# Squares kept in memory by 32 rows, in runs of 512 bytes (attention and mixture of experts, one core)

## The chip, the core and the metric

The kernel runs on one core of one Trainium2 chip. The metric is device time in microseconds, the median of several executions of the compiled program. The engines are named as in the profile: PE multiplies matrices, DVE (VectorE) and ACT (ScalarE) work element by element, POOL scatters rows, and SP issues nearly all DMA transfers from one queue that it works off in order. A core has 16 DMA engines, and all transfers share them.

## The reference

```python
# 8 batches, S = 2496 rows, u and v 256 wide, z 64 wide
scores = matmul(z, z.transpose(0, 2, 1)) / S
attn = maximum(scores, 0.0) ** 2
x = (u * matmul(attn, v)).reshape(8 * 2496, 256)
logits = x @ w_gate + modality_bias[modality_id]     # 8 experts
e_idx = argmax(logits, axis=1)                       # one expert for each row
out[rows of e] = gate * (maximum(x @ w1[e], 0) @ w2[e])   # 256 -> 1024 -> 256, gate = softmax at e
```

The scores are z times its own transpose, so `attn` is symmetric: the squares of one block above the diagonal are those of the mirrored block below it, turned.

## The kernel before, in words

**Tiles.** A batch's 2496 columns (queries) are cut into five column chunks, four of T = 512 and a last one of 448 (`NCH`, `LAST`). The text calls them columns 0 to 4. The rows (keys) are taken two tiles of 128 at a time: ten steps i = 0 to 9 (`NI`) for each column, key chunk i // 2, its first or second half i % 2. The host interleaves keys so that partition p holds keys 2p and 2p + 1 of a half. `steps` lists (batch, column, i), 400 in all, in the order in which `order_of` mixes them.

**A step.** Fresh steps multiply z with z on PE (`scores`, L334), take relu and scale on ACT (`root`, L345), and square on ACT (`square`, L394). This gives `a`, 128 partitions x 2 key tiles x 512 queries in float32. `a` is split for the multiplication into a high part `ah` (`high`, L418, on DVE or ACT, whichever the scheduler finds free) and a low part `al` (`low`, L427, on DVE; L429 and L430 in the last step), and `weigh` (L451) adds ah·vh, ah·vl and al·vh into PSUM, 24 half-height matmuls a step. `ah` and `al` have `DEPTH` = 4 buffers each, `a` has `NA` = 6.

**Turned steps.** Where the mirrored block was made in an earlier column of the batch, it is not made again. The earlier step is a source (`is_source`): `turn_squares` (L364) transposes `a` in 32 x 32 blocks on DVE into one of two `turn` buffers, `store_squares` (L377, L381) writes it to memory, and the later step's `load_turned` (L354) reads it back as its `a`. Column c makes 8 - 2c full source steps and reads 2c turned ones. Below column 4 there is also a half step on the diagonal: its upper 256 queries are made (`root` writes them into the tile that `load_turned` filled), its lower 256 come from memory, stored by the step before it (i == 2c). In the last batch fewer pairs are turned.

**Layout in memory before.** `squares[q, c, e]` is 512 x 512 floats, a row for each query of the source. A source step fills 256 of a row's 512 places. Each quarter of 32 partitions goes out in a DMA of its own, 32 x 16 runs of 64 floats (256 bytes). In step 9, whose second key tile is not interleaved, runs are 32 floats (128 bytes) and there are six DMAs. A read takes 128 partitions, each two whole rows: 4096 bytes on end, or two runs of 1792 bytes in the last column, or two of 1024 in a half step.

**What sets the order.** `step_pieces`, `chunk_pieces` and others describe all work as pieces, each with an engine, a cost, a step by which it is needed, what it must follow and which buffers it takes. A list scheduler runs through them at build time with a clock for each engine and issues, for the engine that is furthest behind, the piece with the earliest need that is ready and fits. The recorded order on each engine is fixed then; the chip waits where the costs were wrong. `transfer` makes a piece of SP's queue. Besides squares the queue carries `zr` and `vr` (the next batch's z and v, mostly read in columns 2 and 3), `ut` (u), and in the first batch eight `blank` stores. POOL scatters each batch's rows (`xs`) during columns 1 to 3 of the next.

**Afterwards** (from about 1279 us) the experts run: `up` (L1268), `down_high` (L1279), `down_low` (L1283). They touch none of this.

## Time and profile before

| | |
|---|---|
| median of 3 executions | 2155.69 us (2152.55 to 2157.73) |
| the profiled execution's own time | 2161.44 us |
| its span, first to last instruction | 2159.0 us |
| mean granted PE clock | 0.995 |
| PE, weight loads, DVE, ACT busy | 2128.9, 1900.2, 1650.3, 1422.8 us |
| DMA packets, MB moved | 605497, 373.21 |

The page shows busy time of each engine over the span, and the same in slices. The table of busy time by stretch gives, for a stretch between two times, its length, busy us of PE, of PE's weight loads, DVE, ACT and POOL with their instruction counts, the granted PE clock (1.00 is full), the mean busy share of the 16 DMA engines (over 1 where packets overlap on an engine) and GB/s. Groups of instructions give count, busy us, the mean ns of one, and the idle time just before them with what ended it. The list of waits gives who waited for whom: us in total, times, longest. The chain that ended last is followed back from the last instruction to whatever released each step; its pieces give start and length in us.

### The profile page before, as it was taken

To read this page: it belongs to the slowest core of one execution; us is meant where nothing else is said; L and a number is where in the kernel's file an instruction comes from. 1 tells how busy PE (TensorE), PEld (TensorE's weight loads), DVE (VectorE), ACT (ScalarE), POOL (GpSimd) and SP (SyncE) were. 2 spreads that over 40 slices of the span, in tenths; PEclk is the share of its full clock that TensorE was granted. 3 is DMA by queue.
4 is the path that set the end of the run, shared out by engine and by line. 5 is a ranking of instruction groups with operands and counts; after the bars stand their busy time and mean duration, and the time that the engine had idled before them with its cause. 6 is when DMAs were issued, how large, how long until landed. Compare 5 with 4: busy or idle time off the path is not lost.

```text
span 2159.0 us, 44814 instructions
## 1 busy us (share of the span) xinstructions
PE 2128.9 (99%) x17190; PEld 1900.2 (88%) x17190; DVE 1650.3 (76%) x2292; ACT 1422.8 (66%) x2031; POOL 351.5 (16%) x342
## 2 busy tenths in 40 slices
PE   9999999999999999999999999999999999999997
PEld 7889999989989988888999988888888888888886
DVE  8889888878889889888888876666666666666664
ACT  8668868869768769779778753455455555454553
POOL 0000220210220210210310503112121211112121
PEclk9999999999999999999999999999999999999999
DMA  8976977977877978968968843645454544545451
GB/s 180 260 229 140 236 215 145 233 204 147 222 213 145 232 208 168 240 188 176 251 167 177 240 123 98 179 121 163 127 161 133 145 149 132 161 126 166 120 156 36
DMA packets 605497, 373.21 MB, mean 173 GB/s; under 512 B 522810, under 2 KB 547642, under 8 KB 605274
## 3 DMA queue, kind: packets, MB, share of 16 engines
q1 hardware_dynamic: 590186, 329.06, 60.8%
q0 software_dynamic: 15088, 41.21, 5.1%
q8 instruction: 136, 2.23, 0.4%
q14 instruction: 87, 0.71, 0.1%
HBM read 237.84 MB, written 132.31 MB: 171 GB/s over the span
## 4 chain that ended last, share of the span: by engine, by line
PE 86%; DMA 4%; issue 3%; DVE 3%; ACT 2%; SPq 1%; POOL 0%; POOLq 0%; DVEq 0%; ACTq 0%
PE acc L451 41%; PE ph L1268 18%; PE po L1279 12%; PE s L334 6%; PE po L1283 6%; DMA out_dram<-y,ids 2%; PE po L547 2%; DMA squares<-turn 1%; DMA r<-squares 1%; DVE al L427 1%; SPq L377 1%; ACT r L345 1%; ACT r L394 1%; DVE turn L364 0%; SPq L381 0%
## 5 line engine op out<-in xcount | busy, mean ns | idle before, releaser
L451 PE MATMUL acc<-ah,vh 64*128 64x512 f32 (+1 forms) x3120 | 468.6, 386 | 3.5 <-DVE ah L418 3.3
L451 PE MATMUL acc<-al,vh 64*128 64x512 f32 (+1 forms) x3120 | 456.5, 383 | 3.9 <-DVE al L427 3.9
L451 PE MATMUL acc<-ah,vl 64*128 64x512 f32 (+1 forms) x3120 | 455.9, 383 | 0.0
L427 DVE TENSOR_TENSOR al<-r,ah 128x1024 fp32r<-128x1024 f32 (+1 forms) x359 | 421.4, 1184 | 37.5 <-ACT ah L418 32.4
L1268 PE MATMUL ph<-xh,w 128*128 128x512 f32 x1248 | 399.5, 390 | 0.1
L1273 DVE SCALAR_TENSOR_TENSOR hl<-ph,hh 128x512 fp32r<-128x512 f32 x312 | 211.4, 688 | 236.3 <-ACT hh L1272 209.9
L1272 ACT ACTIVATE hh<-ph 128x512 fp32r<-128x512 f32 x312 | 187.1, 600 | 303.3 <-PE ph L1268 236.1
L671 POOL DMA_INDIRECT xs<-x,sloti x160 | 193.8, 1211 | 1076.4 <-ACT ah L418 492.6
L451 PEld LDWEIGHTS acc<-al,vh 64*128 64x128 f32 x3120 | 342.0, 185 | 28.6 <-DVE al L427 5.1
L451 PEld LDWEIGHTS acc<-ah,vh 64*128 64x128 f32 x3120 | 337.2, 185 | 28.7 <-DVE ah L418 3.7
L451 PEld LDWEIGHTS acc<-ah,vl 64*128 64x128 f32 x3120 | 337.3, 185 | 23.6
L418 ACT CAST ah<-r 128x1024 fp32r<-128x1024 f32 (+1 forms) x281 | 285.7, 1033 | 78.9 <-PE acc L451 46.6
L1279 PE MATMUL po<-w,hh 128*128 128x512 f32 x1248 | 296.7, 389 | 0.0
L345 ACT ACTIVATE r<-s 128x1024 f32<-128x1024 f32 (+2 forms) x244 | 235.7, 967 | 83.8 <-PE s L334 72.4
L1268 PEld LDWEIGHTS ph<-xh,w 128*128 128x128 f32 x1248 | 234.6, 188 | 47.8 <-issue 0.6
L1279 PEld LDWEIGHTS po<-w,hh 128*128 128x128 f32 x1248 | 234.1, 188 | 48.3
L1292 POOL DMA_INDIRECT out_dram<-y,ids x157 | 152.7, 973 | 721.2 <-DVE y L1320 686.2
L364 DVE STREAM_TRANSPOSE turn<-r 128x1024 f32<-128x1024 f32 (+1 forms) x189 | 217.0, 1151 | 41.1 <-DMA squares<-turn 27.6
L394 ACT ACTIVATE r<-r 128x1024 f32<-128x1024 f32 (+2 forms) x243 | 242.8, 999 | 5.7
L1268 PE MATMUL ph<-xl,w 128*128 128x512 f32 x624 | 243.7, 391 | 0.1
L334 PE MATMUL s<-zm 64*128 64x512 f32 (+2 forms) x1452 | 211.9, 383 | 5.2 <-ACT r L345 4.9
L869 DVE TENSOR_TENSOR w<-wq,w 128x1024 fp32r<-128x1024 f32 x148 | 177.8, 1221 | 19.3 <-ACT w L865 19.0
(158 smaller groups left out, 2013.1 us busy)
## 6 DMA issues: line engine op xcount, KB each, us to landing
wq<-in_moe_w_dram SPq DMA_DIRECT2D x148, 512.0 KB
squares<-turn SPq DMA_DIRECT2D x508, 128.0 KB
r<-squares SPq DMA_DIRECT2D x96, 512.0 KB
r<-squares SPq DMA_DIRECT2D x62, 448.0 KB
ut<-in_ut_dram SPq DMA_DIRECT2D x40, 512.0 KB
xg<-xs SPq DMA_DIRECT2D x156, 128.0 KB
squares<-turn SPq DMA_DIRECT2D x310, 64.0 KB
vr<-in_v_dram SPq DMA_DIRECT2D x32, 512.0 KB
```

Source lines behind the costliest of these rows:

```text
L334: nc.tensor.matmul(out=s[t][:, w], lhsT=lhs, rhs=mv[halves[t], ql, w], start=n == 0, stop=n == 2)
L345: nc.scalar.activation(out=r[:, t, w], in_=s[t][:, w] if g < 2 else s[:, :, w], func=AF.Relu, scale=INV)
L364: nc.vector.transpose(out=y.rearrange(order, n=2)[:, :, t], in_=x[:, :, t])
L394: nc.scalar.square(out=a[:, t, w], in_=r[:, t, w])
L418: copy(out=ah[:, :, :w], in_=st_a[g][:, :, :w])
L427: nc.vector.tensor_tensor(out=al[:, :, :w], in0=a[:, :, :w], in1=ah[:, :, :w].bitcast(F32), op=ALU.subtract)
L451: nc.tensor.matmul(out=acc[b, c][r][dh][:, :w], lhsT=V[b, k // J][y][halves[r], k % J, dh * P:(dh + 1) * P], rhs=x[halves[r], k % 2, :w], ...
L671: nc.gpsimd.indirect_dma_start(out=xs, out_offset=bass.IndirectOffsetOnAxis(ap=RT[b]["sloti"][:n, k:k + 1], axis=0), in_=x[:n, j, :], in_o ...
L1268: nc.tensor.matmul(out=ph, lhsT=lhs, rhs=rhs[:, k, :], start=n == 0, stop=n == 3 * KD - 1)
L1272: nc.scalar.activation(out=hh, in_=ph, func=AF.Relu)
L1273: nc.vector.scalar_tensor_tensor(out=hl, in0=ph, scalar=0.0, in1=hh.bitcast(F32), op0=ALU.max, op1=ALU.subtract)
L1279: nc.tensor.matmul(out=po[j], lhsT=x, rhs=both, start=f == 0, stop=False, skip_group_check=True)
```

## The change

`squares[q, c, e]` keeps the same number of floats, now as [2 halves of the source's keys, 4 quarters of 32 partitions, 8 groups, 32 rows, 128 floats]. A source step writes one half; each quarter is one DMA of 32 x 8 runs of 128 floats (512 bytes), four DMAs in every step, the last keys too, and with 32 x 4 runs in the half step. A read is one DMA of 128 partitions with eight runs of 512 bytes (four in a half step); in the last column it is now 512 wide.

A group of 128 floats holds two key tiles of 64 queries each, so a tile read back is not in the order [key tile, query]. `blocks` and `in_blocks` name the two orders, `views` pairs them, and the splits `high` and `low` read the one and write the other. In the last column, whose queries end in two tiles that are not interleaved, `views` gives three pieces, so each split is three instructions (4 x 64, 4 x 32 and 2 x 32 queries of both key tiles). The transposition now takes every second query of a block as it reads and packs differently as it writes; in the half step it is two instructions. The half step's computed part is written and squared in the block order. The scheduler's costs of the transfers are changed.

```diff
-    squares = {(q, c, e): dram.tile([T, T], F32, name=f"squares{q}_{c}_{e}") for q, c in pairs for e in range(2)}
+    squares = {(q, c, e): dram.tile([2, P // BLK, 2 * P // BLK, BLK, P], F32, name=f"squares{q}_{c}_{e}") for q, c in pairs for e in range(2)}
...
     def root(g):
...
         if is_half(g):
             r = st_a[g]
-        else:
-            r = bulk.tile([P, 2, T], F32, tag="a", bufs=NA, name="r") if g else first_root
+            nc.scalar.activation(out=blocks(r)[:, :, H // 64:], in_=in_blocks(s[:, :, w]), func=AF.Relu, scale=INV)
+            st_s[g] = r
+            return
+        r = bulk.tile([P, 2, T], F32, tag="a", bufs=NA, name="r") if g else first_root
...
     def load_turned(g):
         b, c, i = steps[g]
-        w = H if is_half(g) else width[c]
         a = bulk.tile([P, 2, T], F32, tag="a", bufs=NA, name="r")
-        src = squares[i // 2, c, b % 2].rearrange("(s p k) q -> s p k q", s=2, k=2)
-        nc.sync.dma_start(out=a[:, :, :w], in_=src[i % 2, :, :, :w])
+        m = P // BLK
+        src = squares[i // 2, c, b % 2][0:1 if is_half(g) else 2, :, i % 2 * m:(i % 2 + 1) * m].rearrange("s n m i x -> (m i) (s n) x")
+        x = a.rearrange("p k (g x) -> p (k g) x", x=P)
+        nc.sync.dma_start(out=x[:, 0:src.shape[1]], in_=src)
         st_a[g] = a

+    def blocks(a):
+        return a.rearrange("p k t -> p (k t)").rearrange("p (g k w) -> p k g w", k=2, w=64)
+    def in_blocks(x):
+        return x.rearrange("p k (g w) -> p k g w", w=64)
+    def views(g, a, *split):
+        _, c, i = steps[g]
+        w = width[c]
+        if not is_turned(g) and not is_half(g):
+            return [[x[:, :, :w] for x in (a, *split)]]
+        y = blocks(a)
+        if c < NCH - 1:
+            return [[y] + [in_blocks(x) for x in split]]
+        at = [slice(0, H), slice(H, H + P), slice(H + P, w)]
+        parts = [y[:, :, 0:4], y[:, :, 4:8, 0:BLK], y[:, :, 4:6, BLK:]]
+        return [[v] + [x[:, :, t].rearrange("p k (g w) -> p k g w", g=v.shape[2]) for x in split] for v, t in zip(parts, at)]

     def turn_squares(g):
-        y = raw.tile([P, T // BLK, 2 * BLK], F32, tag="turn", bufs=2, name="turn")
-        order = "p t (i n) -> p n t i" if i < NI - 1 else "p t (n i) -> p n t i"
-        t = slice(H // BLK if i == 2 * c else 0, T // BLK)
-        x = st_a[g].rearrange("p n (t i) -> p n t i", i=BLK)
-        nc.vector.transpose(out=y.rearrange(order, n=2)[:, :, t], in_=x[:, :, t])
+        y = raw.tile([P, 2 * P // BLK, P], F32, tag="turn", bufs=2, name="turn")
+        order = "p g (k i n) -> p n g k i" if i < NI - 1 else "p g (k n i) -> p n g k i"
+        some = slice(P // BLK if i == 2 * c else 0, 2 * P // BLK)
+        x = st_a[g].rearrange("p n (g i k) -> p n g k i", i=BLK, k=2)
+        turned_to = y.rearrange(order, n=2, i=BLK)
+        if i == 2 * c:
+            for n in range(2):
+                nc.vector.transpose(out=turned_to[:, n, some], in_=x[:, n, some])
+        else:
+            nc.vector.transpose(out=turned_to, in_=x)

     def store_squares(g):
...
         for n in range(P // BLK):
-            mine = y[n * BLK:(n + 1) * BLK]
-            if i < NI - 1:
-                k0 = i % 2 * H + n * 2 * BLK
-                t = slice(H // BLK if i == 2 * c else 0, T // BLK)
-                nc.sync.dma_start(out=dst[:, t, k0:k0 + 2 * BLK], in_=mine[:, t])
-            else:
-                for k in range(2 if n < 2 else 1):
-                    k0 = (J // 2 + k) * P + n * BLK
-                    nc.sync.dma_start(out=dst[:, :, k0:k0 + BLK], in_=mine[:, :, k * BLK:(k + 1) * BLK])
+            nc.sync.dma_start(out=dst[n, some].rearrange("g i x -> i g x"), in_=y[n * BLK:(n + 1) * BLK, some])
...
     def high(g):
...
-        copy(out=ah[:, :, :w], in_=st_a[g][:, :, :w])
+        for x, y in views(g, st_a[g], ah):
+            copy(out=y, in_=x)
...
     def low(g):
...
-            nc.vector.tensor_tensor(out=al[:, :, :w], in0=a[:, :, :w], in1=ah[:, :, :w].bitcast(F32), op=ALU.subtract)
+            for x, h, y in views(g, a, ah, al):
+                nc.vector.tensor_tensor(out=y, in0=x, in1=h.bitcast(F32), op=ALU.subtract)
...
-            read = transfer(0.7 if is_half(n) else 1.4, n - LEAD - (4 if is_half(n) else 2.5), load_turned, n, after=src, take=[hold_a], gate=n - LEAD - (6.0 if is_half(n) else 4))
+            read = transfer(1.0 if is_half(n) else 1.9, n - LEAD - (4 if is_half(n) else 2.5), load_turned, n, after=src, take=[hold_a], gate=n - LEAD - (6.0 if is_half(n) else 4))
...
-                stored[b, c, i] = transfer(1.4 if i == 2 * c else 2.8, n - 1.4 if i == 2 * c else n + 0.4, store_squares, n, issues=4 if i < NI - 1 else 6, after=[t])
+                stored[b, c, i] = transfer(1.0 if i == 2 * c else 1.9, n - 1.4 if i == 2 * c else n + 0.4, store_squares, n, issues=4, after=[t])
```

Two places show how the recorded order moves. The first is SP's queue in the first batch, where column 2 ends and column 3 begins. `squares_3_0_88` and the like name blocks: the first figure is the column that reads them, the second the batch's parity; `r` is the tile read into, `turn` the tile stored from. Before:

```order
L354 DMA r<-squares_3_0_88 128x1024
L354 DMA r<-squares_3_0_80 128x1024
L381 DMA squares_4_0_64<-turn 32x16x32 x6
L377 DMA squares_3_0_84<-turn 32x8x64 x4
L152 DMA xs<-blank 128x1032
L354 DMA r<-squares_3_0_80 128x1024
L354 DMA r<-squares_4_0_68 128x2x448
L266 DMA ut<-in_ut_dram 128x1024
L158 DMA vr<-in_v_dram 128x1024
L354 DMA r<-squares_4_0_68 128x2x448
L354 DMA r<-squares_3_0_84 128x2x256
L377 DMA squares_4_0_70<-turn 32x16x64 x4
```

The same place after:

```order
L357 DMA r<-squares_3_0_80 128x8x128
L402 DMA squares_4_0_64<-turn 32x8x128 x4
L152 DMA xs<-blank 128x1032
L357 DMA r<-squares_3_0_80 128x8x128
L158 DMA vr<-in_v_dram 128x1024
L402 DMA squares_3_0_84<-turn 32x4x128 x4
L357 DMA r<-squares_4_0_68 128x8x128
L266 DMA ut<-in_ut_dram 128x1024
L357 DMA r<-squares_4_0_68 128x8x128
L402 DMA squares_4_0_70<-turn 32x8x128 x4
L357 DMA r<-squares_3_0_84 128x4x128
```

The store of the last keys has become four DMAs where it was six; the load of `vr` has moved ahead of the half step's store (`squares_3_0_84<-turn`), and the half step's read (`r<-squares_3_0_84`) stands behind the next step's store instead of ahead of it.

The second place is DVE in the last column of the second batch, where it makes low parts (`al`) and some of the high ones (`ah`). Before:

```order
L427 TENSOR_TENSOR al<-r,ah 128x2x448 x2
L669 COPY x<-side 128x2
L418 CAST ah<-r 128x2x448
L427 TENSOR_TENSOR al<-r,ah 128x2x448
L418 CAST ah<-r 128x2x448
L427 TENSOR_TENSOR al<-r,ah 128x2x448
```

After:

```order
L452 TENSOR_TENSOR al<-r,ah 128x2x256
L452 TENSOR_TENSOR al<-r,ah 128x2x128
L452 TENSOR_TENSOR al<-r,ah 128x2x64
L694 COPY x<-side 128x2
L442 CAST ah<-r 128x2x256
L442 CAST ah<-r 128x2x128
L442 CAST ah<-r 128x2x64
L452 TENSOR_TENSOR al<-r,ah 128x2x256
L452 TENSOR_TENSOR al<-r,ah 128x2x128
L452 TENSOR_TENSOR al<-r,ah 128x2x64
```

Each instruction of 448 queries on both key tiles has become three, of 256, 128 and 64; the order among the steps is the same.

More of the change, by code (lines that the diff above doesn't have):

```diff
@@ L370, in store_squares @@
         y = st_t.pop(g)
-        dst = squares[c, i // 2, b % 2].rearrange("(t i) k -> i t k", i=BLK)
+        some = slice(P // BLK if i == 2 * c else 0, 2 * P // BLK)
+        dst = squares[c, i // 2, b % 2][i % 2]
         for n in range(P // BLK):
-            mine = y[n * BLK:(n + 1) * BLK]
-            if i < NI - 1:
-                k0 = i % 2 * H + n * 2 * BLK
-                t = slice(H // BLK if i == 2 * c else 0, T // BLK)
-                nc.sync.dma_start(out=dst[:, t, k0:k0 + 2 * BLK], in_=mine[:, t])
-            else:
-                for k in range(2 if n < 2 else 1):
-                    k0 = (J // 2 + k) * P + n * BLK
-                    nc.sync.dma_start(out=dst[:, :, k0:k0 + BLK], in_=mine[:, :, k * BLK:(k + 1) * BLK])
+            nc.sync.dma_start(out=dst[n, some].rearrange("g i x -> i g x"), in_=y[n * BLK:(n + 1) * BLK, some])
     roots = {}
@@ L391, in square @@
             roots[g] = r
-        for t in (range(2),) if g else ((0,), (1,)):
-            t = slice(t[0], t[-1] + 1)
-            nc.scalar.square(out=a[:, t, w], in_=r[:, t, w])
+        if is_half(g):
+            nc.scalar.square(out=a[:, 1, :], in_=r[:, 1, :])
+        else:
+            for t in (range(2),) if g else ((0,), (1,)):
+                t = slice(t[0], t[-1] + 1)
+                nc.scalar.square(out=a[:, t, w], in_=r[:, t, w])
         st_a[g] = a
@@ L414, in high @@
             return first_high(g)
-        w = width[steps[g][1]]
         ah = bulk.tile([P, 2, T], F32R, tag="ah", bufs=DEPTH, name="ah")
         copy = {"D": nc.vector.tensor_copy, "A": nc.scalar.copy}[by[g]]
-        copy(out=ah[:, :, :w], in_=st_a[g][:, :, :w])
+        for x, y in views(g, st_a[g], ah):
+            copy(out=y, in_=x)
         st_h[g] = ah
```

## The prediction

> **What bounds the kernel now.** I read the page first: how busy TensorE (PE) is, and what its DMA engines carry.
>
> ```profile
> PE 2128.9 (99%) x17190; PEld 1900.2 (88%) x17190; DVE 1650.3 (76%) x2292; ACT 1422.8 (66%) x2031; POOL 351.5 (16%) x342
> DMA packets 605497, 373.21 MB, mean 173 GB/s; under 512 B 522810, under 2 KB 547642, under 8 KB 605274
> HBM read 237.84 MB, written 132.31 MB: 171 GB/s over the span
> ```
>
> PE is idle for 2159.0 - 2128.9 = 30.1 us. The change leaves all matmuls alone, so only idle time (and the clock after it) can be won. Next the table of busy time by stretch, for the places where PE idles (length, then busy us of PE, weight load, DVE, ACT, POOL; granted clock; DMA share):
>
> ```profile
> 0.00:60.00 60.00, 56.28 (x456) 44.61 (x458) 49.81 (x74) 50.87 (x58) 3.05 (x18) 1.00 0.82 183
> 130.00:136.00 6.00, 2.75 (x26) 1.95 (x24) 1.88 (x3) 4.48 (x7) 0.00 (x0) 1.00 1.05 322
> 440.00:450.00 10.00, 7.14 (x85) 6.64 (x82) 3.71 (x6) 5.18 (x7) 1.94 (x2) 1.00 1.01 322
> 590.00:600.00 10.00, 7.19 (x52) 6.10 (x50) 6.10 (x10) 4.13 (x6) 3.17 (x2) 0.85 1.06 250
> 760.00:770.00 10.00, 7.87 (x107) 6.73 (x105) 7.93 (x11) 6.74 (x11) 2.98 (x2) 1.00 0.99 350
> 2078.00:2159.00 81.00, 69.41 (x357) 58.73 (x355) 41.74 (x60) 34.51 (x54) 13.93 (x15) 0.95 0.24 79
> ```
>
> The start (3.7) and the tail (11.6) I leave as they are: there the first loads and the last rows of output set the time. Four stalls lose 3.25 + 2.86 + 2.81 + 2.13 = 11.05 us, each with the DMA engines full (0.99 to 1.06). The chain that ended last names what they waited for:
>
> ```profile
> 127.60 7.35 DMA r<-squares
> 441.63 6.44 DMA r<-squares
> 587.27 7.77 DMA squares<-turn
> 743.87 7.25 DMA xs<-x,sloti
> ```
>
> Two are squares read back, one a store that frees a turn buffer. The list of waits agrees (us, times, longest):
>
> ```profile
> DVE turn L364 <- DMA squares<-turn: 27.6, 21, 3.6
> ACT ah L418 <- DMA r<-squares: 21.9, 13, 4.7
> DVE ah L418 <- DMA r<-squares: 4.1, 1, 4.1
> ```
>
> Last, one whole batch (the fifth), column by column, 0 to 4:
>
> ```profile
> 655.00:688.00 33.00, 33.00 (x332) 29.77 (x332) 30.33 (x36) 26.65 (x37) 0.00 (x0) 1.00 0.81 155
> 688.00:721.00 33.00, 33.00 (x334) 32.17 (x332) 32.21 (x54) 27.73 (x41) 1.20 (x1) 1.00 0.77 163
> 721.00:752.00 31.00, 31.00 (x317) 30.68 (x315) 26.17 (x35) 23.20 (x31) 11.82 (x10) 1.00 1.01 281
> 752.00:784.00 32.00, 29.86 (x304) 26.33 (x302) 25.62 (x35) 16.11 (x26) 11.19 (x10) 1.00 0.95 273
> 784.00:812.00 28.00, 28.00 (x314) 25.46 (x314) 25.49 (x30) 22.77 (x34) 1.04 (x2) 1.00 0.48 127
> ```
>
> DMA is full in columns 2 and 3 (1.01, 0.95), loose in 0 and 1, half empty in 4; PE loses its time in column 3. What the change does to the DMA load of columns 2 and 3 decides.
>
> **The DMA runs.** Issues before (count, KB each):
>
> ```profile
> squares<-turn SPq DMA_DIRECT2D x508, 128.0 KB
> r<-squares SPq DMA_DIRECT2D x96, 512.0 KB
> r<-squares SPq DMA_DIRECT2D x62, 448.0 KB
> squares<-turn SPq DMA_DIRECT2D x310, 64.0 KB
> r<-squares SPq DMA_DIRECT2D x31, 256.0 KB
> ```
>
> By the code the 508 stores write 512 runs of 256 B each; of the 310, 124 write 256 runs of 256 B and 186 (last keys) 512 runs of 128 B: 387,072 runs. The reads take 128 runs of 4096 B, 256 of 1792 B and 256 of 1024 B: 36,096. After, 158 full steps and 31 half ones write and read 1024 or 512 runs of 512 B: 177,664 each way. Runs fall from 423,168 to 355,328; bytes each way rise from 86.9 to 91.0 MB, since the last column's reads become 512 wide.
>
> No trace row shows a 512 B run. I bound it from two stretches with different mixes, the hardware queue's row first of 671 to 704 us and then of 721 to 752 us (packets, MB, share of 16 engines):
>
> ```profile
> q1 hardware_dynamic: 15828, 5.19, 78.8%
> ```
> ```profile
> q1 hardware_dynamic: 12012, 7.36, 88.0%
> ```
>
> 0.788 x 16 x 33 us / 15828 = 26.3 ns at 328 B a packet; 0.880 x 16 x 31 / 12012 = 36.3 ns at 613 B. The line through them is 14.8 ns a run plus 0.0352 ns a byte: 19.3 ns at 128 B, 23.8 at 256, 32.8 at 512, 50.8 at 1024, 77.9 at 1792, 159 at 4096. So, in us of all 16 engines:
>
> - a full store: 2048 x 23.8 / 16 = 3.05, now 1024 x 32.8 / 16 = 2.10: -0.95; with the last keys 3072 x 19.3 / 16 = 3.71, now 2.10: -1.61; a half step 1.52, now 1.05: -0.47;
> - a full read: 128 x 159 / 16 = 1.27, now 2.10: +0.83; in the last column 1.25, now 2.10: +0.85; a half read +0.24.
>
> Column c stores 8 - 2c full steps (one with the last keys) and, below column 4, a half step, and reads 2c full ones and a half. Column 0: 7 x -0.95 - 1.6 - 0.5 + 0.2 = -8.5. Column 1: -6.8 + 1.9 = -4.9. Column 2: -4.9 + 3.6 = -1.4. Column 3: -3.0 + 5.2 = +2.2. Column 4: 8 x 0.85 = +6.8. Over the kernel 774 us become 728. So the saving lies where DMA has room; columns 2 and 3 together stay (+0.8 of 63 us), column 2 is relieved by 1.4 and column 3 loaded with 2.2. The fifth batch's stall comes 8 to 18 us into column 3 (752; 760 to 770), when column 2's relief counts whole and column 3's load in part. I take 1.0 to 1.4 us less queue ahead of each of the four late transfers: -4 to -5.6, with a little of the clock (0.85 granted in one of those windows). The ends: all four go (-11), or the +2.2 lands on them.
>
> SP's queue: 72 issues fewer (last keys, six to four). It is in order, and a read that waits for its stores holds up all behind it; shorter stores shorten that.
>
> **The engines.** Groups that keep shapes apart (count, busy, mean ns):
>
> ```profile
> L364 DVE STREAM_TRANSPOSE turn<-r 128x1024 f32<-128x1024 f32 x158 | 195.4, 1239 | 27.7 <-DMA squares<-turn 17.0 <-ACT r L394 6.1 <-issue 4.0
> L427 DVE TENSOR_TENSOR al<-r,ah 128x896 fp32r<-128x896 f32 x72 | 76.8, 1086 | 4.7 <-ACT ah L418 3.0 <-PE acc L451 0.6
> L888 DVE STREAM_TRANSPOSE xt<-xg 128x1024 f32<-128x1024 f32 x39 | 48.2, 1235 | 0.0
> L511 DVE TENSOR_TENSOR x<-acc,x 128x512 f32<-128x512 f32 x64 | 41.3, 682 | 3.6 <-ACT x L507 3.6
> L233 DVE TENSOR_TENSOR zm<-zr,zm 128x512 fp32r<-128x512 f32 x40 | 27.5, 687 | 5.8 <-ACT zm L228 5.5
> L418 DVE CAST ah<-r 128x896 fp32r<-128x896 f32 x35 | 21.5, 630 | 8.4 <-PE acc L451 5.9 <-ACT r L394 2.6
> L511 DVE TENSOR_TENSOR x<-acc,x 128x128 f32<-128x128 f32 x16 | 4.5, 280 | 0.0
> ```
>
> The transposition now reads every second float; before, it wrote so, at 1239 ns, against 1235 for one with neither. L511 reads every second float of PSUM at 682 ns, against 687 for L233 that reads runs. I take zero; the upper end is double.
>
> In the last column each split is three instructions (512, 256, 128 elements). From 1086 ns at 896 and 280 at 128 an instruction costs 146 ns beside its elements: two more are +0.29 us. Eight low parts a batch are +2.3, and some three of the high ones that DVE makes +0.9 (bounded by the same 146, since the 630 is a faster form). That is 3.2 us where DVE is idle 28.00 - 25.49 = 2.5 while PE never waits. Uncovered it is 0.7 us a batch, 5 in all; PE's queue of four split buffers hides it, so I take zero. ACT idles 5.2 us there and gains some two instructions on each of five casts, 1 to 2 us. The half step's transposition becomes two, +0.13 us by the same fit. All other splits are as long as before, in another order.
>
> **Sum.** -4 to -5.6 from the stalls, zero from the engines: -5. The profiled execution (span 2159.0, 2.4 more around it, 2161.4) becomes 2156.4; it lies 5.7 above the median of the runs shown, 2155.69, which becomes 2150.7.
>
> **Rivals.**
>
> - *The new order gives it back.* The list scheduler takes other costs (reads 1.4 to 1.9, stores 2.8 to 1.9), and a few swaps in the SP queue decide whether a batch stalls: only batches with late transfers in column 3 do. For: the first batch's half read of column 3 now stands behind one more store. Within 4 us of 2155.7.
> - *The reads become the bound* (slower). Column 3's extra 2.2 us meet engines that are 0.95 busy in a stretch with 32 us; 0.95 x 32 + 2.2 = 32.6 is past full. Once the queue is still full when column 3's own reads stand in it, each batch that stalls now loses 2.2 more and the others begin to: four to seven batches, +9 to +15. Likeliest +9: 2165. Against: column 2 sheds 1.4 first. The Trainium skill, "DMA: Bandwidth & Descriptors", section "Why small descriptors are slow (HBM only)", speaks for it: every run carries a fixed overhead. The 14.8 ns a run of the line above agree.
> - *All stalls go*, if a 512 B run costs far less than 32.8 ns, say the 128 B price, 19.3. A full read is then 1.24, as now, a store 1.24, and columns 2 and 3 lose some 14 us of load. -11 of stalls and, with the clock, up to -18: 2138. The same page, "Specifications", gives 512 B as the least size for line rate and says that shorter ones are read, modified and written; by its 27 GiB/s an engine a run would take about 18 ns (an estimate), which would give this result. The trace contradicts the reading part: HBM was read for 237.84 MB, which the loads account for, with none left for stores that first read.
> - *DVE becomes the bound* (far slower). Columns 0 and 1 leave DVE 2.67 + 0.79 = 3.5 us; 16 transpositions pass that from 0.22 us more each. At double, 16 x 1.24 - 3.5 = 16 us a batch, +120: 2275.
>
> **Chances.** Forecast (-1 to -10) 0.42, order 0.22, reads 0.24, all stalls 0.08, DVE 0.04. A measurement of this kernel can tell about 0.2% (4.3 us) from no change. Faster by more: 0.35 of the forecast's 0.42 and 0.08 make 0.43. Within: 0.22 and the forecast's 0.07, 0.29. Slower: 0.28. The range goes from all stalls gone (2138) to the reads at +10 (2166); outside lie DVE, the upper part of the reads and the lowest of the stalls, under 0.2.
>
> **What would show it.** Packets fall by some 68,000 to 537,700, those under 512 B by 387,072 to 135,700; if not, the runs are not what I count. DMA share in column 4 rises from 0.48 to about 0.7, in column 0 falls from 0.81 to about 0.55, in columns 2 and 3 it stays near 1. Transpositions keep 1239 ns. The waits of the turn on stores fall from 27.6 us, those on squares read back stay near 26. I am wrong if the stalls of columns 2 and 3 change by more than 8 us either way, or if PE idles in columns 0 or 4.

## The result, and the profile after

The changed kernel takes 2139.87 us, the median of 6 runs (2138.04 to 2142.05); the kernel before took 2153.65 us in 6 runs beside it (2152.12 to 2157.73). The ratio is 0.9934 (95% interval 0.9921 to 0.9947): 13.8 us or 0.66% faster. The profiled execution's own time is 2142.05 us with a span of 2140.0. It is the longest of its six, and that of before (2161.44) lay above all six beside which the change was measured, so the two profiles differ by more than the medians do.

The page of the changed kernel, busy time and DMA:

```profile
PE 2120.3 (99%) x17190; PEld 1927.7 (90%) x17190; DVE 1656.9 (77%) x2483; ACT 1437.1 (67%) x2119; POOL 354.6 (17%) x342
DMA packets 536667, 381.35 MB, mean 178 GB/s; under 512 B 134746, under 2 KB 491098, under 8 KB 536442
q1 hardware_dynamic: 521354, 337.19, 58.3%
HBM read 241.90 MB, written 136.38 MB: 177 GB/s over the span
```

PE's idle time is 2140.0 - 2120.3 = 19.7 us, 10.4 less than the 30.1 of before. The span fell by 19.0. So the other 8.6 us came off PE's *busy* time, with the same 17190 matmuls. More than half of that is the clock. The table of busy time by stretch shows how a stall costs twice. First the kernel before: behind the first batch's stall, from the middle of the third batch's on, and behind the fourth's (length, busy us of PE, weight load, DVE, ACT, POOL; granted clock; DMA share; GB/s):

```profile
135.00:140.00 5.00, 4.18 (x22) 3.33 (x24) 4.87 (x7) 2.35 (x3) 0.00 (x0) 0.66 0.62 153
445.00:450.00 5.00, 2.14 (x19) 1.80 (x16) 0.77 (x1) 1.85 (x2) 0.00 (x0) 1.00 1.04 374
450.00:455.00 5.00, 4.21 (x40) 3.66 (x41) 2.60 (x5) 3.36 (x11) 1.75 (x2) 0.53 0.99 274
455.00:460.00 5.00, 5.00 (x38) 4.44 (x36) 3.75 (x6) 2.78 (x4) 1.59 (x2) 0.79 0.89 225
595.00:605.00 10.00, 7.91 (x56) 6.45 (x58) 9.78 (x13) 3.90 (x4) 3.42 (x3) 0.83 1.05 278
```

In the third batch PE idles for 2.86 us up to 450 us and for 0.79 us more behind it, 3.65 in all. Then it works at a granted clock of 0.53 and 0.79, which loses 5 x 0.47 + 5 x 0.21 = 3.4 us of clock in 10 us. Behind the first and the fourth batch's stalls 5 x 0.34 and 10 x 0.17 lose 1.7 us each; behind the fifth's the clock stays at 1.00. The Trainium skill, "TensorE: Matmul & The Clock Gate", section "Part 1: The HAM clock gate (the "warmup" mystery)", says that an idle window of about 3.4 us puts the array at half rate until it has been busy as long. The trace agrees with the half rate (0.53), but less idle time was enough here: the first and the fourth batch's stalls have 3.25 and 2.81 us. The fifth's, with 2.13 us, did not do it.

The same places in the changed kernel, and its start and tail:

```profile
130.00:136.00 6.00, 6.00 (x56) 4.83 (x54) 5.64 (x7) 5.60 (x11) 0.00 (x0) 1.00 0.57 161
436.00:444.00 8.00, 5.38 (x57) 4.64 (x55) 3.38 (x5) 5.12 (x12) 1.25 (x2) 0.87 1.10 313
441.00:446.00 5.00, 5.00 (x51) 4.43 (x49) 2.74 (x7) 4.27 (x8) 1.94 (x2) 0.66 1.07 299
590.00:600.00 10.00, 10.00 (x132) 9.84 (x130) 6.36 (x9) 6.54 (x15) 2.91 (x3) 1.00 1.00 270
760.00:770.00 10.00, 10.00 (x97) 10.00 (x95) 8.13 (x20) 4.36 (x11) 1.16 (x2) 1.00 0.76 205
0.00:60.00 60.00, 56.38 (x474) 44.72 (x474) 50.54 (x75) 51.92 (x59) 3.04 (x18) 1.00 0.80 202
2060.00:2140.00 80.00, 68.39 (x352) 57.89 (x350) 41.23 (x59) 34.05 (x54) 13.21 (x14) 0.95 0.22 75
```

Three of the four stalls are gone whole; that of the third batch is left, some 10 us earlier, with 8.00 - 5.38 = 2.62 us of the 11.05. (The 11.05 cut the third batch's stall at 450 us; with the whole 3.65 the four had 11.84.) Of the 6.8 us of clock lost behind them 5 x 0.34 = 1.7 are left, so the clock gave 5.1 of the 8.6 us. The rest is not explained by these rows; part of it lies ahead of all stalls, where PE does 474 matmuls in the first 60 us in place of 456, at a clock of 1.00 both times. Start (3.6) and tail (11.6) idle as they did. The chain that ended last names the transfer behind the stall that is left, a square read back, and the list of waits (us, times, longest) shows both kinds of wait on the squares down:

```profile
431.65 6.31 DMA r<-squares
```
```profile
DVE turn L392 <- DMA squares<-turn: 13.3, 10, 2.8
ACT ah L442 <- DMA r<-squares: 10.1, 6, 3.6
DVE turn L390 <- DMA squares<-turn: 4.4, 5, 1.7
```

Waits for turn buffers: 27.6 to 13.3 + 4.4 = 17.7 us; for squares read back: 21.9 + 4.1 to 10.1. Last the fifth batch by column:

```profile
637.00:672.00 35.00, 35.00 (x352) 34.83 (x350) 30.52 (x36) 33.12 (x47) 0.00 (x0) 1.00 0.74 172
672.00:704.00 32.00, 32.00 (x327) 31.68 (x325) 30.69 (x52) 28.39 (x39) 1.24 (x2) 1.00 0.67 169
704.00:735.00 31.00, 31.00 (x317) 30.68 (x315) 25.76 (x37) 23.83 (x32) 13.08 (x11) 1.00 0.99 296
735.00:765.00 30.00, 30.00 (x309) 29.84 (x307) 22.92 (x38) 20.78 (x36) 9.14 (x9) 1.00 1.03 302
765.00:793.00 28.00, 28.00 (x313) 27.77 (x312) 26.15 (x45) 23.25 (x40) 0.00 (x0) 1.00 0.36 100
```

DMA is as full in columns 2 and 3 as before (0.99 and 1.03), yet PE no longer waits there, and column 4 is emptier (0.36 against 0.48). A full queue shows a share of 1 however long it is. That it became shorter shows where it runs dry, behind the stretch and not in it.

### The profile page after: what moved, and what is told of

The parts are those of the page before. It is cut to its first block, busy times and chain, and to the rows that moved or that the text cites. A ratio compares the mean times of both kernels' runs of the same rounds, so it can differ in the third digit from the quotient of the medians.

```text
span 2140.0 us, 45015 instructions
## 1 busy us (share of the span) xinstructions
PE 2120.3 (99%) x17190; PEld 1927.7 (90%) x17190; DVE 1656.9 (77%) x2483; ACT 1437.1 (67%) x2119; POOL 354.6 (17%) x342
## 3 DMA queue, kind: packets, MB, share of 16 engines
q8 instruction: 136, 2.23, 0.4%
HBM read 241.90 MB, written 136.38 MB: 177 GB/s over the span
## 4 chain that ended last, share of the span: by engine, by line
PE 88%; DMA 4%; issue 2%; DVE 2%; ACT 2%; SPq 1%; POOL 0%; POOLq 0%; DVEq 0%; ACTq 0%
PE acc L476 43%; PE ph L1293 19%; PE po L1304 12%; PE po L1308 6%; PE s L334 6%; DMA out_dram<-y,ids 2%; PE po L572 2%; DMA squares<-turn 1%; DMA vr<-in_v_dram 1%; ACT r L347 1%; ACT r L418 1%; DVE al L452 1%; DVE turn L392 1%; SPq L402 0%; DMA r<-squares 0%
## 5 line engine op out<-in xcount | busy, mean ns | idle before, releaser
L476 PE MATMUL acc<-ah,vh 64*128 64x512 f32 (+1 forms) x3120 | 484.8, 385 | 0.8 <-DVE ah L425 0.8
L476 PE MATMUL acc<-ah,vl 64*128 64x512 f32 (+1 forms) x3120 | 473.5, 382 | 0.0
L452 DVE TENSOR_TENSOR al<-r,ah 128x1024 fp32r<-128x1024 f32 (+4 forms) x483 | 429.9, 922 | 32.7 <-ACT ah L442 29.8
L476 PEld LDWEIGHTS acc<-al,vh 64*128 64x128 f32 x3120 | 364.5, 184 | 14.1 <-DVE al L452 0.6
L476 PEld LDWEIGHTS acc<-ah,vh 64*128 64x128 f32 x3120 | 360.3, 185 | 16.4 <-DVE ah L425 1.3
L476 PEld LDWEIGHTS acc<-ah,vl 64*128 64x128 f32 x3120 | 361.3, 184 | 14.1
L442 ACT CAST ah<-r 128x1024 fp32r<-128x1024 f32 (+4 forms) x369 | 299.4, 846 | 56.0 <-PE acc L476 41.3
L347 ACT ACTIVATE r<-s 128x1024 f32<-128x1024 f32 (+2 forms) x213 | 217.0, 1020 | 74.1 <-PE s L334 66.0
L418 ACT ACTIVATE r<-r 128x1024 f32<-128x1024 f32 (+2 forms) x212 | 222.7, 1051 | 5.2
L392 DVE STREAM_TRANSPOSE turn<-r 128x1024 f32<-128x1024 f32 x158 | 195.8, 1241 | 32.9 <-ACT r L418 18.0
```

The lines of the kernel that those rows point to most:

```text
L347: nc.scalar.activation(out=r[:, t, w], in_=s[t][:, w] if g < 2 else s[:, :, w], func=AF.Relu, scale=INV)
L392: nc.vector.transpose(out=turned_to, in_=x)
L418: nc.scalar.square(out=a[:, t, w], in_=r[:, t, w])
L442: copy(out=y, in_=x)
L452: nc.vector.tensor_tensor(out=y, in0=x, in1=h.bitcast(F32), op=ALU.subtract)
L476: nc.tensor.matmul(out=acc[b, c][r][dh][:, :w], lhsT=V[b, k // J][y][halves[r], k % J, dh * P:(dh + 1) * P], rhs=x[halves[r], k % 2, :w], ...
```

## The experiments

Theory A: the squares' transfers load one queue, which is full in columns 2 and 3 of each batch; the shorter stores take load from it, and the late transfers come earlier. Rivals: the scheduler's new order did it (B); the gain comes through the transposition, which waits less for its turn buffers (C); it comes from the fewer issues on SP's queue (D). Each ratio below is against runs of the kernel before on the same chip (medians there 2153 to 2157 us). "Recorded load" is the packet time of the hardware queue q1: its share times the span, in us of all 16 engines, good to about 1 us by the rounding of the share. For the kernel before it is 0.608 x 2159.0 = 1312.7, by this row of its page (packets, MB, share):

```profile
q1 hardware_dynamic: 590186, 329.06, 60.8%
```

### Layout or order

**`e1_old_order`**: the new layout with the scheduler's old costs, which give the old order:

```diff
-    read = transfer(1.0 if is_half(n) else 1.9, ...)
+    read = transfer(0.7 if is_half(n) else 1.4, ...)
-    stored[b, c, i] = transfer(1.0 if i == 2 * c else 1.9, ..., issues=4, ...)
+    stored[b, c, i] = transfer(1.4 if i == 2 * c else 2.8, ..., issues=4 if i < NI - 1 else 6, ...)
```

> The new layout (512-byte runs, turned blocks, splits in three pieces) with the scheduler's old transfer costs, so that every engine's recorded order is that of the kernel before. Theory 'load' (the shorter queue of column 2 takes the stalls away, as the prediction has it): the four stalls shrink as they did in the changed kernel, 2138 to 2144 us. Theory 'order' (the stalls went because the scheduler, given other costs, queued the transfers otherwise): batches 0, 2, 3 and 4 stall in column 3 again, 2150 to 2156 us.

Measured: 2143.6 us, ratio 0.9938 (0.9925 to 0.9951).

**`e2_new_order`**: the old layout with the new costs (the same edit the other way in the kernel before):

> The layout of before (runs of 256 and 128 bytes, reads of 4096) with the changed costs of the scheduler, so that every engine's recorded order is that of the changed kernel. Load: no gain, 2150 to 2157 us, PE idle in columns 2 and 3 as before. Order: the time of the changed kernel, 2138 to 2143 us.

Measured: 2167.47 us, ratio 1.0056 (1.0042 to 1.0070). Its waits:

```profile
DVE turn L364 <- DMA squares<-turn: 49.9, 40, 4.4
ACT ah L418 <- DMA r<-squares: 22.3, 9, 4.4
```

B is out: the layout alone brings all of the gain that can be told apart (0.9938 against 0.9934), and the new order on the old layout costs 12 us, which neither theory expected.

**`e4_costs_2p2`**: a third set of costs on the new layout (2.2 and 1.1 us in place of 1.9 and 1.0, for reads and stores alike):

```diff
-    read = transfer(1.0 if is_half(n) else 1.9, ...)
+    read = transfer(1.1 if is_half(n) else 2.2, ...)
-    stored[b, c, i] = transfer(1.0 if i == 2 * c else 1.9, ...)
+    stored[b, c, i] = transfer(1.1 if i == 2 * c else 2.2, ...)
```

> The changed kernel with the scheduler's cost of a full read and a full store at 2.2 us where it has 1.9 (half: 1.1, was 1.0); the layout is the same, the recorded order another. Load: the load is the same, 2137 to 2143 us. Order: another order stalls elsewhere, anything from 2134 (no stall left in the third batch, whose pattern in SP's queue is now that of the batches that do not stall) to 2150 us.

Measured: 2145.93 us, ratio 0.9950 (0.9937 to 0.9963). Its stretches where the first and the third batch stalled:

```profile
130.00:132.00 2.00, 0.17 (x2) 0.00 (x0) 0.00 (x0) 0.00 (x0) 0.00 (x0) 1.00 1.03 344
132.00:134.00 2.00, 0.46 (x4) 0.42 (x6) 0.48 (x1) 1.56 (x2) 0.00 (x0) 1.00 0.09 35
436.00:444.00 8.00, 8.00 (x113) 7.84 (x110) 6.54 (x10) 4.60 (x12) 1.95 (x2) 1.00 1.06 302
```

The third batch's stall is gone and the first batch has one again. It is of a full queue as well: the chain has a square read back from 128.10 us for 4.27 us, and DMA is at 1.03 until it lands and at 0.09 behind it. What stands ahead of a late transfer is a matter of the order too, which so decides over single stalls.

### Load put back

**`e3_more_stores`**: the changed kernel with one quarter of each full source step of columns 2 and 3 stored a second time, to memory that nobody reads:

```diff
+    spare = {...}
...
+        if c in (2, 3) and i > 2 * c:
+            nc.sync.dma_start(out=spare[b, c, i].rearrange("g i x -> i g x"), in_=y[0:BLK])
```

> The changed kernel, its order kept, with one more DMA of 128 KB for each of the six full source steps of columns 2 and 3 (a quarter of the tile stored a second time, to memory that nobody reads). At 32.8 ns a run each adds 256 x 32.8 / 16 = 0.5 us of all DMA engines, some 3 us a batch where they are full, about the load that the rival of longer reads spoke of. Load: stalls come back in several batches, 2146 to 2155 us. Order: the queue's sequence decides and not 3 us of load, 2140 to 2143 us.

Measured: 2150.97 us, ratio 0.9977 (0.9966 to 0.9988). The hardware queue's row on its page and a wait:

```profile
q1 hardware_dynamic: 533866, 343.22, 58.9%
```
```profile
ACT ah L448 <- DMA r<-squares: 17.5, 7, 3.0
```

Recorded load rises from 0.583 x 2140.0 = 1247.6 to 0.589 x 2147.4 = 1264.8 us, 2.2 us a batch, and 0.43% of the gain's 0.66% is given back; waits for squares read back grow from 10.1 to 17.5 us. This speaks for A. But the extra stores also hold the turn buffers, and the transposition waits 7.9 + 2.0 = 9.9 us for them, so this run alone does not part A from C.

### The price of short runs in reads

The prediction charged 0.83 us for a full read in 512 B runs. **`e5_long_reads`**: the changed kernel with its full reads in 128 runs of 4096 B:

```diff
-        x = a.rearrange("p k (g x) -> p (k g) x", x=P)
-        nc.sync.dma_start(out=x[:, 0:src.shape[1]], in_=src)
+        if is_half(g):
+            x = a.rearrange("p k (g x) -> p (k g) x", x=P)
+            nc.sync.dma_start(out=x[:, 0:src.shape[1]], in_=src)
+        else:
+            whole = squares[i // 2, c, b % 2][1].rearrange("n g (a b) x -> (n g a) (b x)", b=8)
+            nc.sync.dma_start(out=a.rearrange("p k t -> p (k t)"), in_=whole)
```

> The changed kernel, with each full read of a block as 128 runs of 4096 B (it takes the whole second half of its block, so some of the data lands in wrong places) in place of 1024 runs of 512 B; half reads, stores and the order of every engine are unchanged. By the prediction's price, 0.83 us more for a read in 512 B runs, some ten reads a batch give 8 us of queue time back in columns 1 to 3, the stall that is left in the third batch goes, and the time falls to 2134 to 2138 us. By the rival that the short runs of the reads cost little here (0.3 us or less), the time stays at that of the changed kernel, 2137 to 2142 us.

Measured: 2138.85 us, ratio 0.9939 (0.9926 to 0.9952): no different from the changed kernel. (Values in wrong places do not change the work: the experts take 879.4 us in both profiles.) The profile does show the transfers coming earlier, in the waits and in the third batch's stretch:

```profile
ACT ah L446 <- DMA r<-squares: 4.0, 2, 2.1
```
```profile
436.00:444.00 8.00, 7.20 (x84) 5.87 (x82) 4.71 (x8) 7.00 (x14) 1.94 (x2) 1.00 1.04 391
```

The waits fall from 10.1 to 4.0 us and the stall that was left from 2.62 to 0.80, so the last stall nearly went, as the dear price foretold; the time does not show it.

**`e6_short_reads`**: the kernel before with its full reads of columns 1 to 3 in runs of 512 B:

```diff
-        nc.sync.dma_start(out=a[:, :, :w], in_=src[i % 2, :, :, :w])
+        if is_half(g) or c == NCH - 1:
+            nc.sync.dma_start(out=a[:, :, :w], in_=src[i % 2, :, :, :w])
+        else:
+            rows_of = squares[i // 2, c, b % 2][i % 2 * H:(i % 2 + 1) * H]
+            runs = rows_of.rearrange("t (c x) -> (t c) x", x=P).rearrange("(j p) x -> p j x", p=P)
+            nc.sync.dma_start(out=a.rearrange("p k (g x) -> p (k g) x", x=P), in_=runs)
```

> The kernel before, with its full reads of columns 1 to 3 cut into runs of 512 B (some of the data lands in wrong places); stores and the order of every engine are unchanged. By the prediction's price, 0.83 us for each of some ten reads a batch, the time grows by 8 to 20 us, to 2163 to 2175. By the rival price, 0.3 us or less, it grows by 0 to 5 us, to 2154 to 2160.

Measured: 2171.33 us, ratio 1.0086 (1.0073 to 1.0099), some 18 us slower. The queue's rows of the two pages (packets, MB, share), long reads first, and the waits with short ones:

```profile
q1 hardware_dynamic: 379786, 337.19, 56.6%
```
```profile
q1 hardware_dynamic: 676202, 329.06, 61.0%
```
```profile
ACT ah L423 <- DMA r<-squares: 30.8, 17, 7.3
DVE turn L369 <- DMA squares<-turn: 29.9, 24, 4.0
```

With the long reads, recorded load falls from 1247.6 to 0.566 x 2136.7 = 1209.4, 0.24 us for each of 158 full reads. With the short ones it rises from 1312.7 to 0.610 x 2165.2 = 1320.8, 0.08 us for each of 96. Neither is 0.83. But the 18 us were what 0.83 had led to expect, so no one price fits both runs: short reads are dear on the old layout, and on the new one they cost nothing that the time can tell. A queue with no slack and one with slack would do this, which fits A but is argued and not shown; and the recorded load, up by 1.0 us a batch, is less than the time, up by 2.3.

### The turn buffers

**`e7_three_turns`**: the kernel before with a third turn buffer:

```diff
-        y = raw.tile([P, T // BLK, 2 * BLK], F32, tag="turn", bufs=2, name="turn")
+        y = raw.tile([P, T // BLK, 2 * BLK], F32, tag="turn", bufs=3, name="turn")
```

> The kernel before, with a third turn buffer in the core's memory and the order of every engine unchanged. If the gain of the shorter stores comes through the transposition, which waits 27.6 us for a turn buffer that a store still reads, a third buffer brings 5 to 10 us as well: 2144 to 2149. If it comes through the load on the DMA queue, which a third buffer leaves as it is, the time changes by 3 us at most: 2151 to 2157.

Measured: 2150.91 us, ratio 0.9989 (0.9979 to 1.0000). Its waits for squares, in the list:

```profile
ACT ah L418 <- DMA r<-squares: 30.4, 15, 4.3
...
DVE turn L364 <- DMA squares<-turn: 1.2, 2, 0.8
DVE ah L418 <- DMA r<-squares: 1.0, 1, 1.0
```

Of the 27.6 us of waiting for buffers 1.2 are left, for 2 us of time (an interval that reaches 1.0000): what ended there is waited for at the squares read back, 26.0 to 31.4 us. C is out as the main cause.

### The last keys: runs or issues

**`e8_last_keys`**: the kernel before with the stores of the last keys as four DMAs in runs of 256 B:

```diff
-        order = "p t (i n) -> p n t i" if i < NI - 1 else "p t (n i) -> p n t i"
+        order = "p t (i n) -> p n t i"
...
-            if i < NI - 1:
+            if True:
```

> The kernel before, with the stores of the last keys as four DMAs of 256 B runs like those of the other keys (their places in the block are permuted), in place of six of which some have runs of 128 B. If the 128 B runs are the dear part of the load, 0.66 us a store by the prediction's rows and some eight such stores a batch, about 5 us of queue time goes from each batch and the stalls shrink by 3 to 8 us: 2146 to 2152. If six DMAs with 128 B runs cost the engines what four with 256 B runs do, no change: 2153 to 2158.

Measured: 2144.07 us, ratio 0.9958 (0.9946 to 0.9971), more than was expected, and with fewer such stores than the expectation counts: 186 DMAs, six to a store, are 31 stores, some four a batch. **`e9_six_of_256`**: the same with six DMAs again:

```diff
-        order = "p t (i n) -> p n t i" if i < NI - 1 else "p t (n i) -> p n t i"
+        order = "p t (i n) -> p n t i"
...
+                k0 = i % 2 * H + n * 2 * BLK
                 for k in range(2 if n < 2 else 1):
-                    k0 = (J // 2 + k) * P + n * BLK
-                    nc.sync.dma_start(out=dst[:, :, k0:k0 + BLK], in_=mine[:, :, k * BLK:(k + 1) * BLK])
+                    t = slice(k * T // BLK // 2, T // BLK if n >= 2 else (k + 1) * T // BLK // 2)
+                    nc.sync.dma_start(out=dst[:, t, k0:k0 + 2 * BLK], in_=mine[:, t])
```

> The kernel before with the stores of the last keys in runs of 256 B, as in e8_last_keys (their places in the block are permuted), but still as six DMAs: two of the four are cut in two. If what e8_last_keys saved is the two issues fewer for each such store on SP's queue, this one is back at the time of the kernel before, 2151 to 2156 us. If it is the 128 B runs themselves, this one is as fast as e8_last_keys, 2142 to 2147.

Measured: 2148.59 us, between the two ranges; ratio 0.9965 (0.9952 to 0.9978). **`e10_six_issues`**: the changed kernel with six DMAs of 512 B runs for the last keys:

```diff
-        for n in range(P // BLK):
-            nc.sync.dma_start(out=dst[n, some].rearrange("g i x -> i g x"), in_=y[n * BLK:(n + 1) * BLK, some])
+        parts = [(n, some) for n in range(P // BLK)]
+        if i == NI - 1:
+            parts = [(n, t) for n in range(2) for t in (slice(0, 4), slice(4, 8))] + parts[2:]
+        for n, t in parts:
+            nc.sync.dma_start(out=dst[n, t].rearrange("g i x -> i g x"), in_=y[n * BLK:(n + 1) * BLK, t])
```

> The changed kernel with two of the four DMAs of each store of the last keys cut in two, so that there are six again, all in runs of 512 B. If the number of issues on SP's queue counts, it loses 4 to 9 us against the changed kernel: 2144 to 2149. If only bytes and runs count, it keeps the changed kernel's time, 2138 to 2143.

Measured: 2145.20 us, in the range that speaks for the issues; ratio 0.9949 (0.9934 to 0.9964). Four DMAs or six: 0.9958 against 0.9965, 0.9934 against 0.9949, each pair with intervals that overlap. An effect of D of 1 to 3 us is not excluded and not shown. A profile of each shows no loss where squares are moved: the experts, which touch none, begin at 1260.6 us in the changed kernel and at 1259.7 with six DMAs, and then take 2140.0 - 1260.6 = 879.4 and 2141.3 - 1259.7 = 881.6 us. The runs of 128 B are shown: with six DMAs on either side, 256 B in their place bring 0.35%, about half of the whole change's 0.66%, though 4.07 MB more are moved. The recorded load does not show it. The queue's row of the kernel with six DMAs of 256 B, and what the 186 issues of these stores took on SP (duration min, median, max in ns; first and last start), with 128 B and then with 256 B:

```profile
q1 hardware_dynamic: 558442, 333.13, 61.2%
```
```profile
L381 SPq DMA_DIRECT2D squares<-turn x186: 303/513/2855, 50.0 to 1225.9; - x186
```
```profile
L382 SPq DMA_DIRECT2D squares<-turn x186: 303/469/1946, 48.5 to 1211.4; - x186
```

0.612 x 2146.3 = 1313.5 us of load, against 1312.7. What differs is how long SP takes to issue such a store: added up in the traces, 126.3 us with 3072 runs a store and 98.5 us with 2048, on average 4.1 and 3.2 us for one of the 31. That what stands behind on the queue comes later by as much is likely, but was not measured.

### The two ways the other way about

**`e11_one_store`**: the changed kernel with a store as one DMA of 128 runs of 4096 B and a read as four of 512 B:

```diff
-    squares = {...: dram.tile([2, P // BLK, 2 * P // BLK, BLK, P], F32, ...)}
+    squares = {...: dram.tile([2, P // BLK, BLK, 2 * P // BLK, P], F32, ...)}
...
+        for k in range(m):
+            nc.sync.dma_start(out=x[k * BLK:(k + 1) * BLK, 0:src.shape[2]], in_=src[i % 2 * m + k])
...
+        nc.sync.dma_start(out=dst.rearrange("n i g x -> (n i) g x")[:, some], in_=y[:, some])
```

> The changed kernel with the square in memory the other way about: a store is one DMA of 128 runs of 4096 B, and a read is four DMAs of 256 runs of 512 B; the number of DMAs, the order of the engines and the bytes are those of the changed kernel. If the load on the engines decides, about as much goes from it as when the reads were made long (some 38 us of all engines over the kernel), most of it in columns 0 and 1, and what is left to win is the last stall and some waits for turn buffers: 2135 to 2140. If the issues on SP's queue decide, a late read now comes with three issues more, 1.3 us or so, in the columns where the queue is full: 2143 to 2150.

Measured: 2145.06 us, ratio 0.9950 (0.9935 to 0.9965). By the median 5 us slower than the changed kernel, but the intervals overlap, and of the 2.9 us between the two profiles 1.7 are lost in the experts, which begin at 1261.8 us here. From its page and its list of waits:

```profile
q1 hardware_dynamic: 367882, 337.19, 56.3%
```
```profile
ACT ah L442 <- DMA r<-squares: 21.2, 10, 5.7
```

Recorded load is the lowest of all (0.563 x 2142.9 = 1206.5 us), yet waits for squares read back double, 10.1 to 21.2 us. The least load of all won nothing; that it went from columns 0 and 1 and not from where it counts is the expectation's account, and was not measured by column. D would explain the later reads, but it was not taken apart from what four DMAs cost otherwise.

### Other load moved out of the full columns

**`e12_late_v`**: the changed kernel with V loaded later:

```diff
-            read = transfer(1.4, need - 7, load_v, b, c, ..., gate=need - 25)
+            read = transfer(1.4, need - 7, load_v, b, c, ..., gate=need - 16)
```

> The changed kernel with one constant of the scheduler altered: the four full loads of V for the next batch, 512 KB each, may go 16 steps ahead of their use in place of 25. They leave columns 2 and 3, where the DMA engines are full, for column 4, where they are not; the squares are stored and read as in the changed kernel, and the order of the engines shifts a little around it. If the load ahead of the late reads decides, some 5 us a batch less in columns 2 and 3 takes the stall of the third batch away (2.8 us and the clock after it) and most of the waits for squares read back (10.1 us): 2134 to 2139 us. If what is left is not the queue's load but the new order's dependencies, the time stays within 2138 to 2143. If the loads come too late in column 4, the first column of the next batch stalls: 2145 or more.

Measured: 2137.45 us (2136.73 to 2137.71), ratio 0.9914 (0.9900 to 0.9928). The page, the third batch's stretch and columns 2 to 4 of the fifth batch:

```profile
PE 2118.7 (99%) x17190; PEld 1901.3 (89%) x17190; DVE 1658.5 (78%) x2481; ACT 1434.2 (67%) x2121; POOL 359.2 (17%) x342
```
```profile
436.00:444.00 8.00, 8.00 (x93) 7.84 (x91) 4.46 (x7) 5.66 (x11) 2.95 (x3) 1.00 1.05 321
...
700.00:731.00 31.00, 31.00 (x317) 30.68 (x315) 26.28 (x38) 21.79 (x30) 13.99 (x12) 1.00 0.89 250
731.00:760.00 29.00, 29.00 (x299) 28.68 (x297) 23.23 (x36) 19.75 (x34) 11.36 (x9) 1.00 0.95 288
760.00:789.00 29.00, 29.00 (x322) 28.77 (x320) 26.67 (x45) 24.25 (x40) 0.51 (x2) 1.00 0.46 134
```

Moving four transfers a batch, with no byte less, ends the last stall. In the changed kernel they stand ahead of the square that PE stalls for: the chain goes from a load of V through a store to that read (431.65 us, above). Its piece, and SP's issues of the four loads in the third batch, first in the changed kernel and then here (duration in ns; first and last start):

```profile
418.81 9.83 DMA vr<-in_v_dram
```
```profile
L158 SPq DMA_DIRECT2D vr<-in_v_dram x4: 357/1977/3209, 408.5 to 429.1; - x4
```
```profile
L158 SPq DMA_DIRECT2D vr<-in_v_dram x4: 1347/2210/3203, 428.2 to 447.0; - x4
```

They come some 16 to 20 us later. They were expected to leave columns 2 and 3 for column 4, and do not: in the fifth batch they are issued from 737.6 to 757.3 us (721.4 to 739.1 in the changed kernel), spread over column 3 in place of the end of column 2 and the start of 3. DMA falls to 0.89 and 0.95 in columns 2 and 3 and rises to 0.46 in column 4, no wait for a square read back is left in the list, and PE's idle time is 2135.5 - 2118.7 = 16.8 us, of which start and tail were 15.2. It is the fastest kernel of the study. Against the changed kernel the intervals touch (0.9928 and 0.9921). Squares, runs and issues are those of the changed kernel, so this is A without the layout: what stands ahead of a late transfer decides. A share may be the order's, which shifted around the loads; above, another order on this layout was worth 1 to 3 us (0.9938 and 0.9950 against 0.9934).

## Why the prediction was right, and what it mis-sized

The direction and its mechanism held: less queue ahead of late transfers in columns 2 and 3, with nothing from the engines. The size did not: -5 us was forecast, -13.8 measured, and by the prediction's own mark (stalls changed by more than 8 us) its working was off: they changed by 8.4, or 9.2 with the third batch's stall whole.

- **The term that failed** is "1.0 to 1.4 us less queue ahead of each of the four late transfers". It came from columns 2 and 3 together keeping their load (+0.8 us), and that from the prices of the line through two stretches. Over the kernel the line gave -46 us; measured is 1247.6 - 1312.7 = -65. Its parts were further off. A full read costs 0.08 to 0.24 us more and not 0.83 to 0.85. At 0.24 all reads cost some 40 us more, so stores save some 105 where the line had 185, 0.57 of it. Column 2 then loses 0.57 x 4.9 = 2.8 and gains 4 x 0.24 + 0.1 = 1.1; column 3 loses 0.57 x 3.0 = 1.7 and gains 6 x 0.24 + 0.1 = 1.5: -1.9 us for both. At 0.08 the stores save 78 (0.42), and both columns change by -2.5. Neither is +0.8. Three stalls of 2.1 to 3.3 us went; 2.2 us a batch put back brought most of the gain's time back.
- **The clock** was a "little" in the forecast. In the profiles it is about 5.1 of 19.0 us: three of the four stalls were followed by a slow clock that lost 1.7 to 3.4 us. Medians differ by less, 13.8 us; the profiled execution of before lay 5.7 us above its median.
- **Load by columns** was wrong for 0 (0.74, not 0.55) and 4 (0.36, not 0.7). Column 4's reads were counted where they are used. In the fifth batch of the changed kernel SP issues 3, 4, 7, 10 and 0 reads in columns 0 to 4 (3, 4, 6, 8 and 3 before), where the prediction counted 1, 3, 5, 7 and 8. So columns 2 and 3 had 14 to 17 reads and not 12; at 0.83 us each these columns would have gained 2.5 to 5 us and not 0.8, which points to slower. That the direction came out right is in part luck: a price that was too high met a count that was too low. SP's issues fell by 62, two for each of 31 stores, and not by 72. Waits for squares read back fell to 10.1 us and did not stay near 26.
- **The engines** went as worked out. The transposition, with the strided read, and its two halves, and the last column's splits in three:

```profile
L392 DVE STREAM_TRANSPOSE turn<-r 128x1024 f32<-128x1024 f32 x158 | 195.8, 1241 | 32.9 <-ACT r L418 18.0 <-DMA squares<-turn 13.3 <-ACT r L414 1.1
L452 DVE TENSOR_TENSOR al<-r,ah 128x512 fp32r<-128x512 f32 x62 | 42.6, 687 | 3.7 <-ACT ah L442 3.1
L452 DVE TENSOR_TENSOR al<-r,ah 128x256 fp32r<-128x256 f32 x62 | 26.1, 421 | 0.0
L390 DVE STREAM_TRANSPOSE turn<-r 128x256 f32<-128x256 f32 x62 | 23.6, 419 | 5.8 <-DMA squares<-turn 4.4 <-ACT r L418 1.2
L452 DVE TENSOR_TENSOR al<-r,ah 128x128 fp32r<-128x128 f32 x62 | 17.9, 288 | 0.0
```

  1241 ns against 1239 (it still writes every second float, and now reads so too); 687 + 421 + 288 = 1396 against 1086, +0.31 (0.29 foreseen); 2 x 419 against 704, +0.13 as foreseen. PE does not wait in column 4.
- **Of the rivals**, DVE falls with the 1241 ns. The order gives nothing back on this layout, but moves a stall from one batch to another and costs 12 us on the old one. "The reads become the bound" has a true mechanism, shown on the old layout (+18 us); here the stores freed more than the reads took. "All stalls go" is what nearly came, though not for its reason: recorded load fell by 65 us in all columns, where 512 B runs at the 128 B price would have taken some 14 us from columns 2 and 3 of every batch, 112 from these alone. Its sentence that the trace contradicts a read before a short write does not follow. The page's 237.84 MB are the sizes of the loads in the list of issues added up, without the 2.23 MB of the instruction queue; a read that a DMA engine made by itself would not stand there. No run here shows whether one is made.
- **What stays open** is the price of short runs beyond the recorded load. While PE stalled, time went with the number of runs: 86,016 runs more cost 18 us, 31,744 fewer won 7.5, the change's 67,840 fewer won 13.8, each 0.20 to 0.24 us for a thousand, though recorded load changed by +8.1, +0.8 and -65.1 us. With most of the stalls gone, 141,568 fewer won nothing that the time can tell; and the 11,776 of the 46 stores put back, which brought bytes and issues too, cost 9 us. That SP is held while it issues many short runs fits this, but was not isolated.

## What to carry to other kernels

Look for the stretch where a queue is full and PE waits, and price a change by the transfers that stand ahead of the late one there: the kernel with the least load of all was no faster, and issuing unrelated transfers some 16 to 20 us later (four loads of V a batch, one constant) ended the stall that the new layout had left. Count runs as well as bytes: a store in 3072 short runs held the issuing engine 4.1 us on average, where 2048 of twice the length took 3.2. And a stall of PE can count nearly double: three of the four were followed by a slow clock that lost 1.7 to 3.4 us more.

## What the runs showed of the hardware

- A transposition of 128 x 1024 floats in 32 x 32 blocks on DVE took 1235 to 1237 ns with no stride, 1239 where it wrote every second float, and 1241 where it also read so (in all but the last keys): the strides are free.
- The recorded packet time of the DMA engines did not rank the kernels. Runs of 256 B in place of 128 B left it as it was (1313.5 against 1312.7 us) and won 7.5 us; long stores and fourfold reads had the lowest (1206.5) and did not beat the changed kernel.
- The page's HBM figures are what the transfers ask for: read were 237.84 MB before and 241.90 after, and the difference is the wider reads of the last column (62 x 64 KB). They cannot tell whether stores in runs under 512 B make memory be read.
- The same eightfold number of runs in a read cost 18 us on the old layout (1.0086) and nothing that the time could tell on the new one (0.9934 against 0.9939 without them).
